# A sparse-attention and feed-forward kernel: a fifth room for raw w2, half of its low parts by GpSimd, and two pieces of w1 asked for later

## The chip, the cores and the metric

The kernel runs on one core of a Trainium2 chip. The metric is the device time of one execution in microseconds; three runs of the kernel before gave 777.71, 779.08 and 780.20 us, median 779.08 us.

## The reference

For 4 batches of 768 tokens and 8 heads of 64, block-sparse attention (blocks of 32 tokens; a query block sees its neighbours, the first and the last block and three sampled ones; the first and the last query block see all), then a feed-forward layer with a residual, all in float32:

```
x   = softmax(mask(q @ k.T / 8)) @ v                  # 3072 rows of 512
xn  = (x - mean) / sqrt(var + 1e-6) * g
out = x + relu(xn @ w1) @ w2                          # w1 512x2048, w2 2048x512
```

## The kernel before, in words

Weights reach the chip as float64 bit patterns. The kernel turns each piece into float32 with three integer passes on VectorE (lines 421, 423, 425), and then into a high and a low float16 part, since every feed-forward product is computed as three float16 matmuls (high by high, low by high, high by low). w1 has 8 pieces of 1 MB (`split_w1`), w2 has 16 of 0.5 MB (`split_w2`).

A piece of w1: VectorE makes the float32, ScalarE scales it in place (L433) and rounds it to the high part (L434), GpSimd subtracts for the low part (L435). A piece of w2: VectorE makes the float32, ScalarE scales and rounds in one step (L431), and VectorE makes the low part (L445, `low_w2`), one piece behind.

Raw pieces and float32 pieces lie in memory that has another use later (lines 405 to 410). Raw w1 has four rooms in the space of w2's parts; raw w2 has four: the second halves of `hh` and `hl` (called `late`) and the two `stg` tiles, which also hold float32 pieces of w1. The float32 pieces of w2 have two rooms, the output tiles `ot`. A load is issued from GpSimd's queue, right after the passes that free its room; the first four pieces of w1 are issued at the start (L508), the first four of w2 in step 2 (L521).

The attention is cut into 60 visits, 15 a batch. At first each pair of visits shares one job, the keys and values of four query blocks: visits 0 and 1 are job 0, 2 and 3 job 1, 4 and 5 job 2; visit 6 is a job of two blocks, and visits 7 to 10 are one job of the first and the last block. One job's transfers on SyncE's queue are, in this order: the band's keys (L144), the values (L180, L188), which must wait until the visits that used that buffer have read it, and twelve gathers of sampled key blocks (L153). The sampled values come by indirect transfers from GpSimd's queue (L192). There are two key and two value buffers.

All engines execute in the order in which the program is written. One pass of the main loop (line 553) is step s. It writes: scores of visit s on TensorE (L203), row maxima on VectorE (`biggest`, L239, L240), attention by values of visit s-1 on TensorE (L274) with its eviction on VectorE (L316 to L322), the exponentials of visit s on ScalarE (L252), and then a list of tasks: the next job's transfers (in even steps at first), the transposes of visit s (`turn`, L264), the weight pieces that `at(step, ...)` put there, and at the end the norm of a finished tile (`norm_a`: L336 to L343 and the subtraction for `xl` on GpSimd, L344). Between the tasks TensorE gets equal portions of the feed-forward work that is due (`run`). The feed-forward begins with step 4. Pieces 0 to 2 of w1 are split before step 0, 3 and 4 in step 0, 5 and 6 in step 1, 7 in step 2; w2 is split four pieces a step in steps 3 to 6.

Of the kernel before, what the change touches and what calls it, by code (L numbers as in the profile page):

```python
# [10 lines left out]
F16 = mybir.dt.float16  # L11
F32 = mybir.dt.float32
I32 = mybir.dt.int32
# [7 lines left out]
SW2 = 64.0  # L21
# [4 lines left out]
def sparse_attention_moe(  # L26
# [13 lines left out]
    nc = tc.nc  # L40
    P = 128
    B = qT.shape[0]
    NB, NR = 24, 3
# [4 lines left out]
    NX, LAG, FFN0 = 5, 1, 3  # L48

    const = ctx.enter_context(tc.tile_pool(name="const", bufs=1))  # L50
    sm = ctx.enter_context(tc.tile_pool(name="sm", bufs=4))
# [5 lines left out]
    def ring(name, n, shape, dtype):  # L57
        return [const.tile(shape, dtype, name=f"{name}{i}") for i in range(n)]
# [3 lines left out]
    w2h = const.tile([P, FT, DM], F16, name="w2h")  # L62
    w2l = const.tile([P, FT, DM], F16, name="w2l")
# [6 lines left out]
    x_s = ring("x", NX, [P, DM], F32)  # L70
# [6 lines left out]
    hl_s = const.tile([P, FT * 2 * P], F16, name="hl")  # L77
    ot_s = ring("ot", 2, [P, DM], F32)
    stg = ring("stg", 2, [P, 2048], F16)
    id_sb = const.tile([P, P], F32, name="id_sb")  # L80
    g_sb = const.tile([P, DM], F32, name="g_sb")
    eps = const.tile([P, 1], F32, name="eps")

    nc.scalar.add_instruction(
        mybir.InstLoadActFuncSet(
            name=nc.get_next_instruction_name(), act_func_set_id=ACT_SET, ins=[], outs=[]
        )
    )

    samp = const.tile([P, 2 * NB * NR], I32, name="samp")  # L90
    bid = const.tile([P, NB + 1], F32, name="bid")
    si = const.tile([P, NB, NR], I32, name="si")
    sf = const.tile([P, NB, NR], F32, name="sf")
    cf = const.tile([P, NB, NR], F32, name="cf")
    tf = const.tile([P, NB, NR], F32, name="tf")
    rf = const.tile([P, NB], F32, name="rf")
    rows = const.tile([P, NB], I32, name="rows")

# [201 lines left out]
    def evict(vi):  # L300
        n = 2 if vi.kind == "D" else 4
        u = vi.pv[:, 0 : n * 65].rearrange("p (h e) -> p h e", e=65)
        if vi.kind == "D":
            half = sm.tile([P, 2, 65], F32, tag="half", name=f"half{vi.i}")
            if not vi.r:
                nc.vector.tensor_copy(half, u)
                vi.half = half
                return
            wt = vi.st[:, 12:16].rearrange("p (r h) -> p r h", r=2).unsqueeze(3)
            nc.vector.tensor_mul(half, u, wt[:, 1].to_broadcast([P, 2, 65]))  # L310
            both = vi.mate.half
            nc.vector.tensor_mul(both, both, wt[:, 0].to_broadcast([P, 2, 65]))
            nc.vector.tensor_add(half, half, both)
            u = half
        rs = sm.tile([P, n, 1], F32, tag="rs", name=f"rs{vi.i}")
        nc.vector.tensor_scalar(out=rs, in0=u[:, :, D : D + 1], scalar1=1e-9, scalar2=None,  # L316
                                op0=ALU.add)
        nc.vector.reciprocal(rs, rs)
        x = vi.tile.x
        if vi.kind == "N":  # L320
            o = x[:, vi.hf * 256 : vi.hf * 256 + 256].rearrange("p (h d) -> p h d", d=D)
            nc.vector.tensor_mul(o, u[:, :, 0:D], rs.to_broadcast([P, 4, D]))  # L322
            return
        for rr in range(2):
            rows = slice(64 * rr, 64 * rr + 64)
            for pp in range(n // 2):
                h = 4 * (vi.hf if vi.kind == "D" else pp) + 2 * rr
                o = x[64:128, h * D : (h + 2) * D] if vi.kind == "D" else x[0:64, h * D : (h + 2) * D]
                nc.vector.tensor_mul(o.rearrange("p (j d) -> p j d", d=D),
                                     u[rows, 2 * pp : 2 * pp + 2, 0:D],  # L330
                                     rs[rows, 2 * pp : 2 * pp + 2, :].to_broadcast([64, 2, D]))
# [72 lines left out]
    split, s = {}, -1  # L404
    late = [x[:, FT * P :] for x in (hh_s, hl_s)]
    w2f, w2g = (x.rearrange("p f e -> p (f e)") for x in (w2h, w2l))
    raw1 = [w2f[:, 0:4096], w2f[:, 4096:8192], w2g[:, 0:4096], w2g[:, 4096:8192]]
    con1 = [stg[0], stg[1], late[0], late[1]]
    raw2 = [late[0], late[1], stg[0], stg[1]]
    con2 = [x.bitcast(F16) for x in ot_s]  # L410

    def load_w1(i, dma):
        dma.dma_start(raw1[i % 4].bitcast(I32), w1[i].bitcast(I32))

    def load_w2(i, dma):
        dma.dma_start(raw2[i % 4].bitcast(I32), w2[i].bitcast(I32))

    def split_w(raw, con, dh, dl, sw):
        raw = raw.bitcast(I32).rearrange("p (e t) -> p e t", t=2)
        wf = con.bitcast(I32)  # L420
        nc.vector.tensor_scalar(out=wf, in0=raw[:, :, 1], scalar1=3, scalar2=0x3FFFFFFF,  # L421
                                op0=ALU.logical_shift_left, op1=ALU.bitwise_and)
        nc.vector.scalar_tensor_tensor(out=wf, in0=raw[:, :, 1], scalar=-0x40000000, in1=wf,  # L423
                                       op0=ALU.bitwise_and, op1=ALU.bitwise_or)
        nc.vector.scalar_tensor_tensor(out=wf, in0=raw[:, :, 0], scalar=29, in1=wf,  # L425
                                       op0=ALU.logical_shift_right, op1=ALU.bitwise_or)
        wf = con.bitcast(F32)
        if len(dh.shape) == 3:
            wf = wf.rearrange("p (c f) -> p c f", c=CT)
        if sw == SW2:  # L430
            nc.scalar.activation(dh, wf, AF.Copy, scale=sw)  # L431
            return
        nc.scalar.activation(wf, wf, AF.Copy, scale=sw)  # L433
        nc.scalar.copy(dh, wf)  # L434
        nc.gpsimd.tensor_sub(dl, wf, dh)  # L435
# [6 lines left out]
            load_w1(i + 4, nc.gpsimd)  # L442

    def low_w2(i):
        nc.vector.scalar_tensor_tensor(out=w2l[:, i, :], in0=con2[i % 2].bitcast(F32), scalar=SW2,  # L445
                                       in1=w2h[:, i, :], op0=ALU.mult, op1=ALU.subtract)
        split[2, i] = s

    def split_w2(i):
        split_w(raw2[i % 4], con2[i % 2], w2h[:, i, :], w2l[:, i, :], SW2)  # L450
        for k in range(max(0, i - 1), i + i // 15):
            low_w2(k)
        if i + 4 < 16:
            load_w2(i + 4, nc.gpsimd)

    tiles, units, visits = [], [], []
    for b in range(B):
# [3 lines left out]
    n = 0  # L461
    while n < len(tiles):
        k = 1 if n == 0 or n == len(tiles) - 1 else 2
# [35 lines left out]
    def at(step, fn, *args):  # L499
        todo.setdefault(step, []).append((fn, args))  # L500
# [4 lines left out]
    nc.scalar.dma_start(bid, blocks)  # L505
    nc.scalar.dma_start(id_sb, eye)
    nc.scalar.dma_start(g_sb, g.to_broadcast([P, DM]))
    for i in range(4):  # L508
        load_w1(i, nc.gpsimd)
    nc.vector.memset(eps, 1e-6)  # L510
    nc.vector.memset(rf, 0.0)
# [2 lines left out]
        pass  # L514
    index_b()
    values(jobs[0])
    for i in range(3):
        split_w1(i)
    for i in range(3, 8):
        at((i - 3) // 2, split_w1, i)  # L520
    for i in range(4):  # L521
        at(2, load_w2, i, nc.gpsimd)
    for i in range(16):
        at(3 + i // 4, split_w2, i)
# [3 lines left out]
    queue, nextu, s = [], 0, 0  # L528
# [24 lines left out]
    while s < NV + LAG + 2 or queue or nextu < len(units):  # L553
        assert s < NV + 60
        vi = visits[s] if s < NV else None
# [27 lines left out]
        if vi:  # L583
# [7 lines left out]
            if queue:  # L591
                k = len(tasks) // 2
# [63 lines left out]
```

## Time and profile before

| what | value |
|---|---|
| median of three runs | 779.08 us |
| the profiled execution, device time | 781.21 us |
| its span, first to last instruction | 779.3 us |
| mean granted TensorE clock | 0.965 |
| busy share TensorE matmul, VectorE, ScalarE, GpSimd | 90%, 42%, 35%, 24% |

Times below are microseconds from the start of the span. PE is TensorE, PEld its weight load, DVE VectorE, ACT ScalarE, POOL GpSimd, SP SyncE, whose queue issues most transfers. L203 is line 203. "[8.25 <-PE ps L203]" behind an instruction says that its engine had been idle for 8.25 us and what ended that. A granted clock of 1.00 is 2.4 GHz, 0.50 is 1.2 GHz.

### The profile page before, as it was taken

Reading aid. Unit: us, or ns where it says so; the run is one execution under the profiler, and the core shown is the slowest. Engines: PE = TensorE matmul, PEld = TensorE weight load, DVE = VectorE, ACT = ScalarE, POOL = GpSimd, SP = SyncE. Lnnn points to the kernel's source line nnn. Section 1 sums busy time; section 2 is a strip of 40 time slices with the busy share of each in tenths; the row PEclk is TensorE's granted clock in tenths of the full one; section 3 lists DMA queues with packets and bytes.
Section 4 is the critical chain, followed back from the end, with each engine's and each line's share of the span. In section 5 each row is a group of like instructions: output and inputs, shape, how many; then the busy total and the mean of one; then the engine's idle time right before and its main releaser. Section 6 shows DMA issues by size and latency. Waiting matters only on the chain.

```text
span 779.3 us, 21817 instructions
## 1 busy us (share of the span) xinstructions
PE 702.4 (90%) x9344; PEld 475.1 (61%) x9344; DVE 326.2 (42%) x658; ACT 271.9 (35%) x561; POOL 188.1 (24%) x220
## 2 busy tenths in 40 slices
PE   0445767999999999999999999999999999999997
PEld 0122653775775775865875856765856857757764
DVE  7577887343351333443432323444332333432211
ACT  2355344343342331443341523343423423342200
POOL 5565211133322203113421103115221012210000
PEclk9967877999999999999999999999999999999999
DMA  8989872767947355569855437379864247431000
GB/s 330 341 251 282 285 247 84 219 184 209 246 131 188 94 167 150 155 165 238 231 153 137 126 129 218 111 194 252 214 167 132 64 147 223 147 87 29 14 29 14
DMA packets 109792, 132.16 MB, mean 170 GB/s; under 512 B 34560, under 2 KB 80896, under 8 KB 108672
## 3 DMA queue, kind: packets, MB, share of 16 engines
q1 hardware_dynamic: 96848, 83.92, 40.5%
q0 software_dynamic: 12416, 46.51, 17.9%
q8 instruction: 74, 1.21, 0.7%
q10 hardware_dynamic: 432, 0.34, 0.1%
q14 instruction: 22, 0.18, 0.1%
HBM read 118.15 MB, written 6.29 MB: 160 GB/s over the span
## 4 chain that ended last, share of the span: by engine, by line
PE 71%; issue 13%; DMA 8%; DVE 5%; POOL 1%; SPq 1%; ACT 1%; POOLq 0%; DVEq 0%
PE pu L367 27%; PE pd L392 25%; PE ps L203 7%; PE pv L274 7%; PE pt L264 6%; DMA ks<-kT 5%; DMA vs<-v 3%; DVE ot L423 1%; DVE w2l L445 1%; DVE ot L421 1%; DMA samp<-sampled 1%; POOL xl L344 0%; DVE st L239 0%; DVE ot L425 0%; SPq L149 0%
## 5 line engine op out<-in xcount | busy, mean ns | idle before, releaser
L367 PEld LDWEIGHTS <-w1h 128*128 128x128 f16 x1664 | 153.6, 99 | 18.1 <-issue 0.2
L252 ACT ACTIVATE p<-ps,st 128x256 f32<-128x256 f32 (+1 forms) x208 | 85.9, 491 | 222.8 <-DVE rs L316 116.4
L392 PE MATMUL pd<-w2h,hl 128*128 128x512 f16 x384 | 147.0, 383 | 0.0
L392 PE MATMUL pd<-w2l,hh 128*128 128x512 f16 x384 | 147.0, 383 | 0.0
L392 PE MATMUL pd<-w2h,hh 128*128 128x512 f16 x384 | 146.9, 383 | 0.0
L378 DVE SCALAR_TENSOR_TENSOR hl<-pu,hh 128x512 f16<-128x512 f32 x96 | 66.4, 692 | 171.2 <-ACT hh L377 170.7
L392 PEld LDWEIGHTS <-hh 128*128 128x128 f16 x768 | 75.2, 99 | 84.7 <-issue 3.0
L367 PE MATMUL pu<-xth,w1h 128*128 128x256 f16 (+1 forms) x832 | 120.9, 267 | 0.0
L367 PE MATMUL pu<-xth,w1l 128*128 128x256 f16 (+1 forms) x832 | 120.9, 267 | 0.0
L367 PE MATMUL pu<-xtl,w1h 128*128 128x256 f16 (+1 forms) x832 | 120.8, 267 | 0.0
L203 PE MATMUL ps<-ks,q 64*32 64x256 f32 (+1 forms) x1664 | 73.5, 418 | 40.3 <-DMA ks<-kT 37.6
L239 DVE TENSOR_REDUCE st<-ps 128x4 f32<-128x1024 f32 (+1 forms) x60 | 69.0, 1151 | 93.5 <-PE ps L203 93.4
L192 POOL DMA_INDIRECT vs<-v,rows x88 | 86.9, 987 | 88.0 <-PE pv L274 49.4
L377 ACT ACTIVATE hh<-pu 128x512 f16<-128x512 f32 x96 | 57.5, 599 | 108.9 <-PE pu L367 108.5
L264 PE MATMUL pt<-id_sb,p 128*128 128x128 f32 x448 | 66.3, 289 | 27.3 <-ACT p L252 23.3
L398 DVE SCALAR_TENSOR_TENSOR ot<-pd,x 128x512 f32<-128x512 f32 x24 | 16.6, 690 | 160.3 <-PE pd L392 160.3
L367 PEld LDWEIGHTS <-w1l 128*128 128x128 f16 x832 | 78.5, 99 | 8.2
L265 ACT COPY pt<-pt 128x512 f32<-128x512 f32 x120 | 61.9, 564 | 61.2 <-PE pt L264 50.7
L264 PEld LDWEIGHTS pt<-id_sb,p 128*128 128x128 f32 x448 | 53.6, 147 | 39.2 <-ACT p L252 28.0
L274 PEld LDWEIGHTS pv<-vs,pt 128*32 128x32 f32 x3584 | 55.6, 110 | 33.9 <-issue 28.4
L400 POOL DMA_DIRECT2D out<-ot x24 | 14.0, 583 | 255.9 <-DVE ot L398 255.9
L203 PEld LDWEIGHTS ps<-ks,q 64*32 64x32 f32 x1664 | 27.1, 109 | 72.0 <-issue 37.1
(83 smaller groups left out, 454.0 us busy)
## 6 DMA issues: line engine op xcount, KB each, us to landing
ks<-kT SPq DMA_DIRECT2D x28, 768.0 KB
ks<-kT SPq DMA_DIRECT2D x264, 64.0 KB
vs<-v SPq DMA_DIRECT2D x20, 780.0 KB
vs<-v SPq DMA_DIRECT2D x4, 1560.0 KB
q<-qT SPq DMA_DIRECT2D x24, 256.0 KB
out<-ot POOLq DMA_DIRECT2D x24, 256.0 KB
vs<-v SPq DMA_DIRECT2D x16, 260.0 KB
w2h<-w POOLq DMA_DIRECT2D x4, 1024.0 KB
```

What stands on the lines that cost most here:

```text
L192: nc.gpsimd.indirect_dma_start(out=vs[:, 2 * gg, :], out_offset=None, in_=src, in_offset=bass.IndirectOffsetOnAxis(ap=rows[:, i : i + 1], ...
L203: nc.tensor.matmul(ps[32 * part : 32 * part + 32, col : col + n], lhs[64 * row : 64 * row + 64], rhs[64 * row : 64 * row + 64], start=True ...
L239: nc.vector.tensor_reduce(out=st[:, 0:n], in_=seen(vi), axis=AX.X, op=ALU.max, negate=True)
L252: nc.scalar.activation(p_s[:, h * w : (h + 1) * w], seen(vi)[:, h, :], AF.Exp, bias=vi.st[:, 4 + h : 5 + h], scale=0.125)
L264: nc.tensor.transpose(pt[:, k - lo, :], p_s[:, k * P : (k + 1) * P], id_sb)
L265: nc.scalar.copy(dst[:, lo:hi, :], pt[:, 0 : hi - lo, :])
L274: nc.tensor.matmul(pv[32 * row : 32 * row + 32, 65 * col : 65 * col + 65], pt[:, ch, 32 * row : 32 * row + 32], vs[:, vv, 65 * e : 65 * e ...
L367: nc.tensor.matmul(ph[:, j * n : (j + 1) * n], w[:, ct, fs], x[:, ct, 0:n], start=m == 0, stop=m == 3 * CT - 1, skip_group_check=True)
L377: nc.scalar.activation(dh, ph, AF.Relu)
L378: nc.vector.scalar_tensor_tensor(out=dl, in0=ph, scalar=0.0, in1=dh, op0=ALU.max, op1=ALU.subtract)
L392: nc.tensor.matmul(po, x[:, f, ts], w[:, f, :], start=m == 0, stop=m == 3 * FT - 1)
L398: nc.vector.scalar_tensor_tensor(out=ot, in0=po, scalar=1.0 / (SW1 * SW2), in1=t.x, op0=ALU.mult, op1=ALU.add)
```

## The change

The index scratch moves into a new 4 KB tile `room`, which afterwards is the fifth room for raw w2. The float32 pieces of w2 get a third room, the last `x` tile. Odd pieces of w2 go the way of w1: ScalarE scales in place and rounds, GpSimd subtracts for the low part; even pieces go as before, with the low part of piece i-1 written by VectorE behind the passes of odd piece i. Two pieces of w1 instead of four are issued at the start, the next two behind the first job's values; two instead of three are split before step 0, then two a step in steps 0 to 2. The first piece of w2 is issued in step 1, the next four in step 2, each later one five pieces ahead. The half sums of the two long query blocks get two fixed tiles.

```diff
@@ -77,8 +77,10 @@
+    room = const.tile([P, 2048], F16, name="room")
+    half_s = ring("half", 2, [P, 2, 65], F32)
@@ -87,12 +89,13 @@
-    samp = const.tile([P, 2 * NB * NR], I32, name="samp")
+    part = room.bitcast(I32)
+    samp = part[:, 0 : 2 * NB * NR]
+    sf, cf, tf = (part[:, (2 + k) * NB * NR : (3 + k) * NB * NR].bitcast(F32)
+                  .rearrange("p (n r) -> p n r", r=NR) for k in range(3))
...
-            half = sm.tile([P, 2, 65], F32, tag="half", name=f"half{vi.i}")
+            half = half_s[vi.r % 2]
@@ -406,16 +409,16 @@
-    raw2 = [late[0], late[1], stg[0], stg[1]]
-    con2 = [x.bitcast(F16) for x in ot_s]
+    raw2 = [room, late[0], late[1], stg[0], stg[1]]
+    con2 = [x.bitcast(F16) for x in (ot_s[0], ot_s[1], x_s[NX - 1])]
...
-        dma.dma_start(raw2[i % 4].bitcast(I32), w2[i].bitcast(I32))
-    def split_w(raw, con, dh, dl, sw):
+        dma.dma_start(raw2[i % 5].bitcast(I32), w2[i].bitcast(I32))
+    def split_w(raw, con, dh, dl, sw, vector=False):
@@ -427,7 +430,7 @@
-        if sw == SW2:
+        if vector:
             nc.scalar.activation(dh, wf, AF.Copy, scale=sw)
             return
         nc.scalar.activation(wf, wf, AF.Copy, scale=sw)
         nc.scalar.copy(dh, wf)
         nc.gpsimd.tensor_sub(dl, wf, dh)
@@ -442,16 +445,19 @@
-        nc.vector.scalar_tensor_tensor(out=w2l[:, i, :], in0=con2[i % 2].bitcast(F32), scalar=SW2,
+        nc.vector.scalar_tensor_tensor(out=w2l[:, i, :], in0=con2[i % 3].bitcast(F32), scalar=SW2,
...
     def split_w2(i):
-        split_w(raw2[i % 4], con2[i % 2], w2h[:, i, :], w2l[:, i, :], SW2)
-        for k in range(max(0, i - 1), i + i // 15):
-            low_w2(k)
-        if i + 4 < 16:
-            load_w2(i + 4, nc.gpsimd)
+        split_w(raw2[i % 5], con2[i % 3], w2h[:, i, :], w2l[:, i, :], SW2,
+                vector=i % 2 == 0)
+        if i % 2:
+            low_w2(i - 1)
+            split[2, i] = s
+        if i + 5 < 16:
+            load_w2(i + 5, nc.gpsimd)
@@ -505,7 +511,7 @@
-    for i in range(4):
+    for i in range(2):
         load_w1(i, nc.gpsimd)
@@ -514,11 +520,14 @@
     index_b()
     values(jobs[0])
-    for i in range(3):
+    for i in range(2, 4):
+        load_w1(i, nc.gpsimd)
+    for i in range(2):
         split_w1(i)
-    for i in range(3, 8):
-        at((i - 3) // 2, split_w1, i)
-    for i in range(4):
+    for i in range(2, 8):
+        at((i - 2) // 2, split_w1, i)
+    at(1, load_w2, 0, nc.gpsimd)
+    for i in range(1, 5):
         at(2, load_w2, i, nc.gpsimd)
```

## Rows read from the trace of the kernel before

**Rows 1.** The page: busy tenths in 40 slices of 19.5 us, and GB/s.

```profile
PE   0445767999999999999999999999999999999997
...
DMA  8989872767947355569855437379864247431000
GB/s 330 341 251 282 285 247 84 219 184 209 246 131 188 94 167 150 155 165 238 231 153 137 126 129 218 111 194 252 214 167 132 64 147 223 147 87 29 14 29 14
```

**Rows 2.** Stretches: length, PE, PEld, DVE, ACT, POOL busy, PEclk, DMA share, GB/s.

```profile
120.00:140.00 20.00, 15.16 (x157) 6.85 (x159) 13.25 (x27) 6.17 (x12) 6.14 (x7) 0.81 0.25 74
140.00:160.00 20.00, 19.92 (x319) 16.43 (x308) 9.00 (x25) 7.78 (x17) 3.00 (x5) 1.00 0.64 181
```

**Rows 3.** Waits from 82 to 140 us: who waited for whom, total, times, longest.

```profile
PE pt L264 <- ACT p L252: 17.5, 3, 9.2
...
DVE hl L378 <- ACT hh L377: 5.7, 4, 3.0
```

**Rows 4.** Timeline of DVE: the row maxima of visits 4 and 7.

```profile
81.36 1.22 DVE L239 TENSOR_REDUCE st<-ps 128x4 f32<-128x1024 f32 x1
...
130.77 0.95 DVE L239 TENSOR_REDUCE st<-ps 128x2 f32<-128x768 f32 x1
```

**Rows 5.** Groups from 70 to 132 us, by form: busy, mean ns, idle before.

```profile
L445 DVE SCALAR_TENSOR_TENSOR w2l<-ot,w2h 128x512 f16<-128x512 f32 x16 | 11.0, 685 | 0.1
L431 ACT ACTIVATE w2h<-ot 128x512 f16<-128x512 f32 x16 | 10.1, 630 | 31.9 <-DVE ot L425 31.9
...
L423 DVE SCALAR_TENSOR_TENSOR ot<-stg,ot 128x512 int32<-128x512 int32 x8 | 5.5, 693 | 0.3
...
L421 DVE TENSOR_SCALAR ot<-stg 128x512 int32<-128x512 int32 x8 | 3.5, 433 | 0.3
```

**Rows 6.** Timeline: subtractions on POOL and the passes of DVE beside them.

```profile
14.10 0.69 DVE L421 TENSOR_SCALAR stg<-w2h 128x1024 int32<-128x1024 int32 x1
...
14.82 1.23 DVE L423 SCALAR_TENSOR_TENSOR stg<-w2h,stg 128x1024 int32<-128x1024 int32 x1
...
16.98 2.31 POOL L435 TENSOR_TENSOR w1l<-stg,w1h 128x1024 f16<-128x1024 f32 x1
17.22 2.62 DVE L421 TENSOR_SCALAR hh<-w2l 128x1024 int32<-128x1024 int32 x1
...
19.87 3.34 DVE L423 SCALAR_TENSOR_TENSOR hh<-w2l,hh 128x1024 int32<-128x1024 int32 x1
19.99 2.14 POOL L435 TENSOR_TENSOR w1l<-stg,w1h 128x1024 f16<-128x1024 f32 x1
...
100.73 1.16 POOL L344 TENSOR_TENSOR xl<-xn,xh 128x512 f16<-128x512 f32 x1 [3.01 <-ACT xh L343]
...
101.17 1.00 DVE L421 TENSOR_SCALAR ot<-hh 128x512 int32<-128x512 int32 x1
```

**Rows 7.** The chain that ended last: start, length, what, up to step 4.

```profile
52.41 4.01 PE ps L203 x32
...
77.70 1.92 PE ps L203 x20
```

**Rows 8.** Timeline of DVE and POOL in steps 0 to 3.

```profile
32.72 1.23 DVE L239 TENSOR_REDUCE st<-ps 128x4 f32<-128x1024 f32 x1 [8.25 <-PE ps L203]
...
56.45 1.22 DVE L239 TENSOR_REDUCE st<-ps 128x4 f32<-128x1024 f32 x1 [5.14 <-PE ps L203]
...
58.53 0.68 DVE L421 TENSOR_SCALAR hl<-w2l 128x1024 int32<-128x1024 int32 x1
...
64.74 1.54 DVE L240 TENSOR_SCALAR st<-st 128x4 f32<-128x4 f32 x1
...
66.19 0.59 POOL L416 DMA_DIRECT2D hh<-w  x1
...
68.39 1.19 POOL L344 TENSOR_TENSOR xl<-xn,xh 128x512 f16<-128x512 f32 x1
...
72.14 0.43 DVE L421 TENSOR_SCALAR ot<-hh 128x512 int32<-128x512 int32 x1 [5.13 <-DMA hh<-w]
```

More of the change, by code (lines that the diff above doesn't have):

```diff
@@ L88, in sparse_attention_moe @@
     )
-    samp = const.tile([P, 2 * NB * NR], I32, name="samp")
+    part = room.bitcast(I32)
+    samp = part[:, 0 : 2 * NB * NR]
+    sf, cf, tf = (part[:, (2 + k) * NB * NR : (3 + k) * NB * NR].bitcast(F32)
+                  .rearrange("p (n r) -> p n r", r=NR) for k in range(3))
     bid = const.tile([P, NB + 1], F32, name="bid")
     si = const.tile([P, NB, NR], I32, name="si")
-    sf = const.tile([P, NB, NR], F32, name="sf")
-    cf = const.tile([P, NB, NR], F32, name="cf")
-    tf = const.tile([P, NB, NR], F32, name="tf")
     rf = const.tile([P, NB], F32, name="rf")
```

## The prediction

> **What bounds the kernel now.** I read the page's slices first: TensorE is busy nine tenths or more from the eighth slice on, about 140 us, and before that at 0 to 7 tenths [rows 1]. The stretches sharpen it: 15.2 of 20 us busy before 140 us, 19.9 of 20 after [rows 2]. So the time is a start of some 140 us and a saturated rest. All feed-forward work in steps 4 to 6 is dealt out by a plan that counts tasks, and the change leaves the number of tasks in those steps alone. TensorE therefore does the same work in the same order, and whatever the start gains or loses moves the end by as much. Removing busy time from an engine after 140 us would be worth nothing.
>
> The start has two stretches. In steps 4 to 6 TensorE waits for the exponentials, 17.5 us in three waits up to 9.2 [rows 3]; those wait for row maxima, and these stand on VectorE behind the four pieces of w2 of the step before. From the maximum of visit 4 to that of visit 7 it is 130.77 - 81.36 = 49.4 us, which VectorE fills [rows 4]. Before that the chain of work runs over transfers: the scores of visit 2 begin at 52.41 and creep for 4.0 us as keys arrive, and the last scores of visit 4 start at 77.70 [rows 7]. The DMA engines are eight or nine tenths busy in the first three slices [rows 1].
>
> **The change, part by part.** Let T2 be the moment when VectorE takes up the maximum of visit 2, 56.45 us now, where it had been idle for 5.14 us waiting for scores [rows 8].
>
> First, the order of the first transfers. It brings the first keys earlier: two pieces fewer stand ahead, 2 MB, and at 341 GB/s [rows 1] that is 6.1 us off the 8.25 us that VectorE waits for the first scores [rows 8]. But T2 hangs on the second job's keys, and by then the same transfers must have landed, all of w1 and both jobs, over engines that are already eight or nine tenths busy. Delayed pieces of w1 come between later keys instead. Three small terms remain: the first piece of w2, now asked for in step 1, adds 0.5 MB, 1.5 us at that rate; while the deferred w1 waits behind the first indirect transfers the queues may run short, up to 2 us; and one piece of w1 may slip behind the keys, -3.1 us. I take T2 1.0 us later, bounds -2.6 and +3.5.
>
> Second, steps 2 and 3. Step 2 now holds two pieces of w1 behind T2 where it held one: three passes, from 14.10 to 17.22, are 3.1 us [rows 6]. They were free before T2, in the idle time; now they aren't. The subtractions of those pieces block VectorE too (next part): now 1.4 us of it lands on the tiny operation after visit 3's maximum (1.54 us) [rows 8]; with two I count 0.6 us more, as part hides behind the norm. So VectorE reaches w2's piece 0 3.7 us later than now. There it waits 5.13 us for the raw piece today, until 72.14 [rows 8]. With that piece loaded in step 1 the wait is gone, and it starts 5.1 - 3.7 = 1.4 us earlier than now. Two things take this back. The `xl` subtraction at 68.39 [rows 8] fell into the idle time, and will fall on passes: 1.1 us. And pieces 1 to 4 are issued behind both subtractions, about 3.8 us later than 66.19; a load took 72.14 - 66.19 = 5.95 us to use [rows 8], so piece 1 comes 66.19 + 3.8 + 5.95 = 75.9, while VectorE is through piece 0 at 70.7 + 1.8 + 1.1 = 73.6. That is a wait of 2.3; with less traffic beside it I take 1.6, bounds 0 and 3. Sum of the part: -1.4 + 1.1 + 1.6 = +1.3.
>
> Third, the low parts. Eight of sixteen leave VectorE: 8 x 0.685 [rows 5] = -5.5 us, all of it inside steps 3 to 6, where VectorE is the path. In their place come eight subtractions on GpSimd. The trace shows what such a one does: while GpSimd subtracts (16.98 and 19.99, 2.31 and 2.14 us) VectorE's first pass takes 2.62 instead of 0.69 and its second 3.34 instead of 1.23, so 1.93 and 2.11 us are lost, nearly the whole subtraction [rows 6]. At the width of w2 one takes 1.16 us, and the pass beside it took 1.00 instead of 0.43, the rest falling on an eviction that reads PSUM [rows 5, 6]. So each costs between 0.57 and 1.16. By place: pieces 1, 5, 9 and 13 have a pass of the next piece right behind, 1.05 each; pieces 3, 7, 11 and 15 end a step, where maxima, norms or a wait for TensorE [rows 3] hide part, 0.6, 0.8, 0.3 and 0.8. Sum 6.7 us, bounds 4.6 and 9.3. The part costs 6.7 - 5.5 = +1.2. If the cover at the ends of steps is gone, it is +3.8.
>
> The Trainium skill, in "SBUF — State Buffer", section "SBUF: two separate sides", says that VectorE and GpSimd share a port pair, held by one instruction for its whole length, while the other blocks fully; it names VectorE's two-port modes and, against a GpSimd operation that reads SBUF, operations with two SBUF inputs. This trace agrees with the block (the 2.62 and 3.34 above). By the full block of 1.16 each the part would be 9.3 - 5.5 = +3.8; by the rows I stay at +1.2.
>
> ScalarE gets one more operation per odd piece, about 0.63 us [rows 5]. I cost it at nothing: it stood idle 31.9 us before those sixteen operations [rows 5]; without that cover it would be 8 x 0.63 = 5.0 us. The third float32 room only spares GpSimd's reader a collision. The fifth raw room buys the early first piece; later pieces have not been late, as the first passes over `stg` were preceded by 0.3 us of idle time in all [rows 5]. The scratch in `room`, the `half` tiles and the even pieces' branch change no instruction's length: nothing. The two deferred loads of w1 now stand on GpSimd's queue ahead of its first subtraction (16.98 [rows 6]), 2 x 0.59 us [rows 8] later for it and for the loads behind it; VectorE's wait of 8.25 us for the first scores covers that, and without it the 1.2 us would fall on the later pieces of w1.
>
> Sum: 1.0 + 1.3 + 1.2 = +3.5 us. The profiled execution, 781.21 us with a span of 779.3, stood 2.1 us over the median; I carry the sum to the median: 779.1 + 3.5 = 782.6 us.
>
> **The rivals.** A measurement of this kernel can tell about 0.3% from no change, 2.3 us: 776.7 to 781.4 is the same.
>
> Slower is my forecast. Its mechanism decides where w2's conversion reaches visit 7's maximum: the loss is there when that row stands later than 130.77.
>
> The keys' lead lasts (faster). If the second job's keys keep the whole 6.1 us that the first gain, the sum is -6.1 + 1.3 + 1.2 = -3.6: 775.5 us. It decides from T2 at 53.95 on, where the 2.5 us of the other two parts are paid. For it speaks that keys and w1 share the engines and the keys are now ahead; against it the engines' shares [rows 1], and that w1's loads still come before T2.
>
> GpSimd works beside VectorE without loss (faster). Then the low parts give -5.5, `xl` costs nothing: 1.0 + 0.2 - 5.5 = -4.3, 774.8 us. Against it stand two rows of 2.62 and 3.34 us [rows 6]; for it, nothing but that those were longer subtractions.
>
> The change does not do what it says (same). The early piece spares 5.13 us and the shorter VectorE work 5.5; if locks hide at 4.6 and the load of piece 1 is in time, with T2 unmoved: 0 - 0.3 - 0.9 = -1.2, 777.9 us. The two moves cancel in a queue that is full anyway.
>
> **How the numbers follow.** Chance for my forecast 0.58, for the lasting lead 0.13, for work without loss 0.06, for cancelling moves 0.23. So faster 0.19, same 0.23, slower 0.58. The forecast's own range comes from its bounds, which will not all fall on one side: 781.4 to 788.5 (T2 at +3.5, the wait at 3, the locks at 9.3 give +3.5 + 2.7 + 3.8 = 10, less the part that can't coincide). With the cases on the other side the range is 775.5 to 788.5.
>
> **What the profile after will show.** Right, if visit 0's maximum comes some 6 us before 32.72 while visit 2's stays within a few us of 56.45; if VectorE passes over 1 us long stand beside subtractions of 1.16 on GpSimd in steps 3 to 6; if the idle time of 5.13 is gone and a shorter one stands before piece 1; and if visit 4's maximum is 2 to 4 us later than 81.36 with the 49.4 us after it about as long. Wrong, if visit 2's maximum comes before 54, if passes keep 0.43 and 0.69 beside GpSimd, or if TensorE's order of work in steps 4 to 6 differs, which would break the rule that the rest only shifts.

## The result, and the profile after

The changed kernel takes 786.35 us in the median (783.66 to 787.75), the kernel before 779.08 us: a ratio of 1.0083 [1.0066, 1.0100], so 5.1 to 7.8 us slower. The profiled execution took 786.49 us with a span of 784.7. The forecast's sign holds, and the time lies in its range of 775.5 to 788.5. Its size does not: +3.5 us was forecast, +6.5 came by the ratio.

The page's first row of slices, TensorE's busy tenths:

```profile
PE   1415557799999999999999999999999999999997
```

The seventh and eighth slices, 117 to 157 us, stand at 7, where the eighth stood at 9 [rows 1]. The two stretches of [rows 2] show the same:

```profile
120.00:140.00 20.00, 14.07 (x216) 7.80 (x205) 16.79 (x29) 9.59 (x19) 4.38 (x6) 1.00 0.46 173
140.00:160.00 20.00, 16.64 (x223) 11.85 (x224) 9.47 (x25) 7.41 (x16) 7.51 (x9) 0.91 0.72 205
```

TensorE is busy for 30.7 of these 40 us instead of 35.1: the saturated part begins later. From visit 8 on nothing more is lost, as the maxima below show, so the whole loss lies in the start.

VectorE's timeline after (start, length, engine, line, operation, out<-in; in brackets the idle time ahead and what ended it). All lines of the changed kernel are some three higher than before.

```profile
22.90 1.23 DVE L242 TENSOR_REDUCE st<-ps 128x4 f32<-128x1024 f32 x1 [5.16 <-PE ps L206]
...
61.01 1.23 DVE L242 TENSOR_REDUCE st<-ps 128x4 f32<-128x1024 f32 x1 [14.50 <-PE ps L206]
...
71.05 1.68 DVE L343 SCALAR_TENSOR_TENSOR xn<-x,ln,g_sb 128x512 f32<-128x512 f32 x1
72.64 1.21 DVE L242 TENSOR_REDUCE st<-ps 128x4 f32<-128x1024 f32 x1
...
75.38 0.42 DVE L424 TENSOR_SCALAR ot<-room 128x512 int32<-128x512 int32 x1
...
78.92 0.43 DVE L424 TENSOR_SCALAR ot<-hh 128x512 int32<-128x512 int32 x1 [0.21 <-DMA hh<-w]
...
82.69 1.52 DVE L428 SCALAR_TENSOR_TENSOR x<-hl,x 128x512 int32<-128x512 int32 x1
...
86.02 0.43 DVE L424 TENSOR_SCALAR ot<-stg 128x512 int32<-128x512 int32 x1 [1.80 <-DMA stg<-w]
...
88.41 1.22 DVE L242 TENSOR_REDUCE st<-ps 128x4 f32<-128x1024 f32 x1
...
97.28 0.69 DVE L381 SCALAR_TENSOR_TENSOR hl<-pu,hh 128x512 f16<-128x512 f32 x1 [6.09 <-ACT hh L380]
...
141.24 0.94 DVE L242 TENSOR_REDUCE st<-ps 128x2 f32<-128x768 f32 x1
```

Visit 0's maximum comes at 22.90 instead of 32.72 [rows 8], 9.8 us earlier. By visit 2 the lead is gone: 61.01 against 56.45, after 14.5 us of waiting for scores.

One trace is not enough to say by how much. The kernel before was profiled a second time (experiment e6 below), and its T2 fell at 59.87, 3.4 us later than in the first trace. The first trace also holds three stands of TensorE, 1.2 us each, between 180 and 560 us, which the second and the changed kernel's don't; so the spans of the two traces shown first differ by 5.4 us only, while visit 8's maximum differs by 8.9. Against the second trace the difference is 6.42 us at visit 8 and 6.21 at the last visit (701.65 and 707.86), so that trace is the one to subtract. By stretches, from the row maxima:

| stretch | before | before, second trace | after | after less second trace | forecast |
|---|---|---|---|---|---|
| start to T2 (visit 2) | 56.45 | 59.87 | 61.01 | +1.1 | +1.0 |
| visit 2 to 3 | 7.03 | 7.53 | 11.63 | +4.1 | +3.7 |
| visit 3 to 4 | 17.88 | 17.32 | 15.77 | -1.6 | -2.1 |
| visit 4 to 7 | 49.41 | 49.22 | 52.83 | +3.6 | +0.9 |
| visit 7 to 8 | 9.74 | 9.02 | 8.14 | -0.9 | 0 |
| sum | 140.51 | 142.96 | 149.38 | +6.4 | +3.5 |

The forecast's terms are laid out by the same stretches: 3.7 is the second piece and its lock; -2.1 is the wait gone, less `xl`, less the wait for piece 1, with two of the eight low parts; 0.9 is the other six. Against this one trace the first three rows come out within 0.6 us; the last is off by 0.9. For T2 that is partly luck. Two more traces share their program up to T2 with one of the kernels: e2 with the kernel before (T2 at 58.88), e5 with the changed one (61.04). The means of 56.45, 58.88 and 59.87 and of 61.01 and 61.04 put T2 some 2.6 us later, not 1.1. The row of visits 4 to 7 is off by 2.7, and the waits from 80 to 145 us say where to look (who waited for whom: total, times, longest):

```profile
PE pt L267 <- ACT p L255: 18.4, 3, 9.2
...
DVE hl L381 <- ACT hh L380: 10.0, 4, 6.1
...
PE pu L370 <- DMA xth<-xh: 5.4, 1, 5.4
...
PE pu L370 <- DMA xtl<-xl: 3.9, 1, 3.9
```

The long waits of TensorE for the exponentials are as before, 18.4 against 17.5 [rows 3]. New are the last two: the first tile's up-projection waits for its own transposed input. VectorE's wait for the result grew from 3.0 [rows 3] to 6.1, and that is 3.1 of the 3.6 us.

Two rows of the chain of work name the transfers, one ahead of T2 and one ahead of that up-projection (start, length, what):

```profile
19.40 34.89 DMA vs<-v
...
78.17 13.55 DMA xtl<-xl
```

In the chain of the kernel before, the first of them is

```profile
28.29 21.23 DMA vs<-v
```

These are values of the second job. They are asked for 8.9 us earlier than before and land at 54.29, 4.8 us later than in the first trace (49.52) and 1.4 us later than in the second (52.89). SyncE's issues of the second job's last keys follow that landing in the chain, and T2 stands 6.7 us behind it, as before (6.9).

### The profile page after: what moved, and what is told of

Same layout as the page of the kernel before. It is cut to its first block, busy times and chain, and to the rows that moved or that the text cites. A ratio compares the mean times of both kernels' runs of the same rounds, so it can differ in the third digit from the quotient of the medians.

```text
span 784.7 us, 21818 instructions
## 1 busy us (share of the span) xinstructions
PE 697.2 (89%) x9344; PEld 475.0 (61%) x9344; DVE 324.2 (41%) x650; ACT 277.4 (35%) x569; POOL 198.4 (25%) x228
## 4 chain that ended last, share of the span: by engine, by line
PE 70%; issue 13%; DMA 8%; DVE 5%; POOL 2%; ACT 1%; SPq 1%; POOLq 0%; ACTq 0%
PE pu L370 27%; PE pd L395 25%; PE pv L277 6%; PE ps L206 6%; PE pt L267 5%; DMA vs<-v 4%; DMA ks<-kT 2%; DMA xtl<-xl 2%; DVE ot L428 1%; DVE ot L426 1%; POOL xl L347 1%; SPq L156 0%; DVE xn L343 0%; DVE w2l L448 0%; DVE st L242 0%
## 5 line engine op out<-in xcount | busy, mean ns | idle before, releaser
L206 PE MATMUL ps<-ks,q 64*32 64x256 f32 (+1 forms) x1664 | 71.0, 418 | 34.6 <-DMA ks<-kT 34.6
L277 PE MATMUL pv<-vs,pt 128*32 128x65 f32 x3584 | 66.2, 226 | 4.5 <-DMA vs<-v 2.8
```

The lines of the kernel that those rows point to most:

```text
L206: nc.tensor.matmul(ps[32 * part : 32 * part + 32, col : col + n], lhs[64 * row : 64 * row + 64], rhs[64 * row : 64 * row + 64], start=True ...
L277: nc.tensor.matmul(pv[32 * row : 32 * row + 32, 65 * col : 65 * col + 65], pt[:, ch, 32 * row : 32 * row + 32], vs[:, vv, 65 * e : 65 * e ...
```

## The experiments

The theory was, at first, the prediction's own: small losses in three places. The largest question was which part of the change carries them. Times are medians against the kernel before, run beside them on the same chip.

**e1: the order of w1 alone.**

```diff
-    for i in range(4):
+    for i in range(2):
         load_w1(i, nc.gpsimd)
...
-    for i in range(3):
+    for i in range(2, 4):
+        load_w1(i, nc.gpsimd)
+    for i in range(2):
         split_w1(i)
-    for i in range(3, 8):
-        at((i - 3) // 2, split_w1, i)
+    for i in range(2, 8):
+        at((i - 2) // 2, split_w1, i)
```

> The kernel before with the w1 order alone changed: two pieces asked for at the start, the next two behind the first job's values, two split before step 0 and two in each of steps 0 to 2. Theory A (the deferred pieces of w1 land among the second job's keys and values): visit 2's maximum moves from 56.45 to 60 to 62 us, and the time is 4 to 8 us over the kernel before. Theory B (the subtractions on GpSimd block VectorE and are the loss): within 2 us of the kernel before, as these are not in it.

785.97 us, ratio 1.0077 [1.0057, 1.0098]: +6.0 us, nearly all of the loss, from the order alone. T2 is at 61.83, visit 3 at 73.46 (11.63 later, as in the changed kernel). Against the second trace of the kernel before, its stretches are +2.0, +4.1, -0.9, +1.0 and -0.7: the second piece behind T2 and the later T2 are the loss. GpSimd's timeline has the loads of the last two pieces of w1, and the chain the values:

```profile
34.56 0.58 POOL L413 DMA_DIRECT2D w2l<-w  x1
...
40.02 0.72 POOL L413 DMA_DIRECT2D w2l<-w  x1
```

```profile
19.84 35.47 DMA vs<-v
```

For e9 below, one more row of e1: its four loads of w2 go out at 75.46 to 77.66, `xtl` at 78.87, and TensorE has it by 86.54, after 7.7 us at most.

```profile
86.54 0.59 PE L367 MATMUL pu<-xtl,w1h 128*128 128x128 f16 x4 [1.99 <-DMA xtl<-xl]
```

**e2: the low parts alone** (odd pieces' low halves by GpSimd, three f32 rooms).

```diff
-    con2 = [x.bitcast(F16) for x in ot_s]
+    con2 = [x.bitcast(F16) for x in (ot_s[0], ot_s[1], x_s[NX - 1])]
...
-        split_w(raw2[i % 4], con2[i % 2], w2h[:, i, :], w2l[:, i, :], SW2)
-        for k in range(max(0, i - 1), i + i // 15):
-            low_w2(k)
+        split_w(raw2[i % 4], con2[i % 3], w2h[:, i, :], w2l[:, i, :], SW2,
+                vector=i % 2 == 0)
+        if i % 2:
+            low_w2(i - 1)
+            split[2, i] = s
```

> The kernel before with the low parts of odd w2 pieces on GpSimd and the third float32 room, nothing else. Theory A: within 2 us of the kernel before, as eight operations of 0.685 us leave VectorE (-5.5) and eight blocks of about 0.8 us each come (5.7 to 6.7). Theory B: 5 to 8 us slower.

778.95 us, ratio 1.0003 [0.9991, 1.0015]: no change, with +1.2 forecast at the upper end of the interval. The lock is there, a subtraction on GpSimd and VectorE's pass beside it:

```profile
80.14 1.28 POOL L435 TENSOR_TENSOR w2l<-ot,w2h 128x512 f16<-128x512 f32 x1 [2.34 <-ACT w2h L434]
```

```profile
80.43 1.53 DVE L425 SCALAR_TENSOR_TENSOR x<-stg,x 128x512 int32<-128x512 int32 x1
```

1.53 instead of 0.69, and 1.52 to 1.54 at pieces 5, 9 and 13. Beside pieces 7 and 15 it is the norm that takes 1.63 instead of 0.75, beside piece 3 the tiny operation after visit 4's maximum, 0.80 instead of 0.36; beside piece 11 nothing is longer. That adds up to 5.6 us. VectorE gives away 8 x 0.685 = 5.5 us [rows 5], and the time agrees.

**e3: the fifth room and the early load alone.**

```diff
-    raw2 = [late[0], late[1], stg[0], stg[1]]
+    raw2 = [room, late[0], late[1], stg[0], stg[1]]
...
-    for i in range(4):
+    at(1, load_w2, 0, nc.gpsimd)
+    for i in range(1, 5):
         at(2, load_w2, i, nc.gpsimd)
```

> The kernel before with the fifth room for raw w2 and its earlier load alone, low parts all on VectorE, the old w1 order. Theory A: the wait of 5.13 us before piece 0 goes, but visit 4's maximum can come no earlier than its scores, 79.6 instead of 81.36, so -2 to +1 us. If the early load instead delays the second job's keys, visit 2's maximum comes 1 to 2 us later and the time is 0 to 3 us longer.

780.47 us, ratio 1.0025 [1.0010, 1.0040], some 2 us slower. The wait of 5.13 [rows 8], 3.4 in the second trace, moves to piece 1 and shrinks to this:

```profile
75.24 0.43 DVE L423 TENSOR_SCALAR ot<-hh 128x512 int32<-128x512 int32 x1 [1.74 <-DMA hh<-w]
```

Yet visit 3 to 4 takes 16.9 us instead of 17.3 to 17.9, and visits 4 to 7 take 50.4 instead of 49.2 to 49.4. What the wait gave is gone before visit 7. T2 is at 59.03, within what the unchanged program shows (56.45 to 59.87), so nothing can be said of the early load's effect on it.

**e4: the changed kernel with the old order of w1** (the reverse of e1's diff, applied to the changed kernel).

> The changed kernel with the old w1 order. Theory A: visit 2's maximum is back within 1 us of 56.45, and the time within 2 us of the kernel before. Theory B: still 5 to 8 us slower than the kernel before.

780.79 us, ratio 1.0022 [1.0010, 1.0035]. The rest of the change costs 1.7 us by itself; with e1's 6.0 that is 7.7, against 6.5 for the whole, which the intervals allow. T2 is at 58.07, not within 1 us of 56.45, but within the spread that e6 shows. Visits 3 to 7 take 68.4 us, against 66.5 and 67.3 in the two traces of the kernel before and 68.6 in the changed kernel. Yet TensorE does not wait for `xth` or `xtl` here: it waits 3.8 us, in two waits, for the third job's keys ahead of visit 4's scores.

**e6: the kernel before once more**, with no edit, profiled a second time.

> The kernel before once more, for a second trace of it. If its start varies from run to run, visit 2's maximum stands somewhere between 56 and 59 us; if the three stands of TensorE of 1.2 us in the first trace (one per batch, in the attention by values of visits 13, 28 and 43) belong to the kernel, they are here again; if to that one execution, they are not.

780.28 us, span 778.5. VectorE's maxima of visits 2, 4 and 7, and the chain's row:

```profile
59.87 1.22 DVE L239 TENSOR_REDUCE st<-ps 128x4 f32<-128x1024 f32 x1 [9.08 <-PE ps L203]
...
84.72 1.22 DVE L239 TENSOR_REDUCE st<-ps 128x4 f32<-128x1024 f32 x1
...
133.94 0.95 DVE L239 TENSOR_REDUCE st<-ps 128x2 f32<-128x768 f32 x1
```

```profile
29.69 23.20 DMA vs<-v
```

The same program, and T2 moves by 3.4 us with the landing of the values (52.89 instead of 49.52). The expected 56 to 59 us was too narrow. That is the uncertainty of any statement on T2 from one trace; whether the execution or the chip makes it was not tried.

**e7 and e8: the two halves of the order.** e7 has the late loads with the old splits, e8 the new splits with the old loads. e7's edit is

```diff
-    for i in range(4):
+    for i in range(2):
         load_w1(i, nc.gpsimd)
...
+    for i in range(2, 4):
+        load_w1(i, nc.gpsimd)
     for i in range(3):
         split_w1(i)
```

> The kernel before with the w1 loads alone moved: two at the start, two behind the first job's values; three pieces are still split before step 0. Theory A (the loads' place is the loss: while only short packets are under way the DMA engines move 250 to 300 GB/s instead of 380 to 420 between 12 and 28 us, and some 1.8 MB less has landed): visit 2's maximum 60 to 63 us, 5 to 9 us slower than the kernel before. Theory C (the splits' place is the loss, a second piece behind visit 2): within 2 us.

And e8:

```diff
-    for i in range(3):
+    for i in range(2):
         split_w1(i)
-    for i in range(3, 8):
-        at((i - 3) // 2, split_w1, i)
+    for i in range(2, 8):
+        at((i - 2) // 2, split_w1, i)
```

> The kernel before with the w1 splits alone moved: four loads at the start as before, but two pieces split before step 0 and two in each of steps 0 to 2. Theory A: visit 2's maximum stays at 56 to 59 us; the second piece behind it costs 3.1 us, of which the wait of 5.1 us before w2's piece 0 hides most if the loads come in time: 0 to 4 us slower. Theory C: 5 to 8 us slower.

e7: 780.62 us, ratio 1.0019 [1.0002, 1.0036], T2 at 58.68, visit 3 at 66.66. e8: 781.12 us, ratio 1.0032 [1.0020, 1.0044], T2 at 56.38, visit 3 at 68.00. Neither half is the loss: e7's theory A and e8's theory C had 5 to 9 and 5 to 8 us. Together (e1) they cost +6.0, by themselves +1.5 and +2.5; the intervals leave room for a plain sum, the traces speak against it. T2 is at 58.68 and 56.38 with one half, at 61.01 and 61.83 with both. In all nine traces of kernels without both halves it lies between 56.38 and 59.87, in all five with both between 61.01 and 64.29. The loads of the last two pieces of w1 on GpSimd, and the values in the chain, stand beside that. In e7:

```profile
37.62 0.57 POOL L413 DMA_DIRECT2D w2l<-w  x1
48.46 0.58 POOL L413 DMA_DIRECT2D w2l<-w  x1
```

```profile
19.77 29.77 DMA vs<-v
```

In e8:

```profile
43.26 0.58 POOL L413 DMA_DIRECT2D w2l<-w  x1
...
45.92 0.76 POOL L413 DMA_DIRECT2D w2l<-w  x1
```

```profile
29.34 16.46 DMA vs<-v
```

With the old splits the last load goes out when the values are nearly in (48.46, landing at 49.54). With the old loads both go out late, at most 2.5 us ahead of the values' landing at 45.80. Only with both edits do two megabytes go out within six microseconds well before that landing, in e1 at 34.56 and 40.02 with the values in at 55.31. So I read that what the order costs at T2 it costs by what it puts side by side at 35 to 52 us, and not by its first 28 us, which e7 shares. That it is these two loads which slow the values is read from five traces (these, the changed kernel and e10) and not shown: a kernel with those two loads alone moved was not tried, and the unchanged program's landing moves by 3.4 us too.

e8 also shows the second piece behind T2 by itself: visit 3 follows T2 by 11.62 us instead of 7.03 and 7.53, 4.1 to 4.6 us.

```profile
56.38 1.22 DVE L239 TENSOR_REDUCE st<-ps 128x4 f32<-128x1024 f32 x1 [4.18 <-PE ps L203]
...
68.00 1.21 DVE L239 TENSOR_REDUCE st<-ps 128x4 f32<-128x1024 f32 x1
```

**e5: the changed kernel, the first tile's norm ahead of four loads of w2** in step 2.

```diff
+    at(2, lambda: norms())
     for i in range(1, 5):
         at(2, load_w2, i, nc.gpsimd)
```

> The changed kernel with the norm of the first tile (with its subtraction on GpSimd and its two transposing transfers) ahead of the four w2 loads of step 2 instead of behind them. Theory D (the transposes, which landed at 91 us, compete with those loads and cost the 3.0 us by which the wait for the first up-projection in step 4 grew, 6.09 against 3.05): 2 to 4 us faster than the changed kernel, 782 to 784 us. If the transposes are late for another reason, within 1 us of the changed kernel's 786.35.

786.45 us, ratio 1.0092 [1.0064, 1.0120]: no gain. `xl` is computed at 74.69 instead of 76.98, and the wait stays (6.58 us), because the transposing transfer is as slow as it was:

```profile
77.98 13.43 DMA xtl<-xl
```

The edit did not do what it was meant to. SyncE issues the transfer behind the third job's gathers and `xth`, at 77.98 instead of 78.17, so it went out no earlier, and the loads of w2, now issued at 75.79 to 77.95, still go beside it. So e5 does not decide on theory D.

The last four were run on another chip, where the kernel before took 782.97 us (779.42 to 785.29). Ratios are to that.

**e9: two loads of w2 beside the transposes instead of four.** The changed kernel with its rooms in another order, so that three pieces of w2 can be asked for in step 1.

```diff
-    raw2 = [room, late[0], late[1], stg[0], stg[1]]
+    raw2 = [room, stg[0], stg[1], late[0], late[1]]
...
-    at(1, load_w2, 0, nc.gpsimd)
-    for i in range(1, 5):
-        at(2, load_w2, i, nc.gpsimd)
+    for i in range(5):
+        at(1 + i // 3, load_w2, i, nc.gpsimd)
```

> The changed kernel with its five rooms in another order (the fifth room, the two stg rooms, the two late rooms), and pieces 0, 1 and 2 of w2 asked for in step 1, pieces 3 and 4 in step 2, so that two loads of w2 instead of four are asked for right ahead of the first tile's transposing DMAs. Theory 'collision' (the wait of 6.1 us for the first normed tile is the transposes' transfer beside the loads of w2): the transposes land about as early as the control's, 78.3 to 80.6 after a like start, the wait of the low normed part falls from 6.1 to about 3 us, and 782 to 784 us. Rival 'the order alone' (the transposes wait for their tile's attention, not for w2): the wait stays at 5 to 6 us, and 785 to 787 us.

VectorE's timeline:

```profile
62.91 1.22 DVE L242 TENSOR_REDUCE st<-ps 128x4 f32<-128x1024 f32 x1 [15.89 <-PE ps L206]
...
94.64 0.69 DVE L381 SCALAR_TENSOR_TENSOR hl<-pu,hh 128x512 f16<-128x512 f32 x1 [3.90 <-ACT hh L380]
```

TensorE's first matmul over `xtl` waited until 91.77 in the changed kernel. Here it has no wait ahead of it:

```profile
85.39 0.63 PE L370 MATMUL pu<-xtl,w1h 128*128 128x128 f16 x4
```

The transfer, issued at 78.90, took 6.5 us at most instead of 13.55. The wait falls from 6.09 to 3.90, visits 4 to 7 take 50.6 us instead of 52.8, and visit 3 to 4 takes 13.4 instead of 15.8. So fewer loads beside it go with a quicker transfer. The four loads alone do not make it slow, as e1 has them too, with 7.7 us; and e10 below has the same 3.90 with all four loads. The time is 789.04 us, ratio 1.0074 [1.0055, 1.0093], not told apart from the change's 1.0083. T2 is 1.9 us later than in the changed kernel's trace, with two more loads on the way by then. Visit 7 to 8 takes 9.8 instead of 8.1, as in all four traces on this chip (9.79 to 9.84), e9's edit or not. Whether the later T2 comes from those loads or from the chance that e6 shows was not tried.

**e10: the changed kernel with one piece less behind T2** (pieces 4, 5 and 6 of w1 in step 1).

```diff
-        at((i - 2) // 2, split_w1, i)
+        at((0, 0, 1, 1, 1, 2)[i - 2], split_w1, i)
```

> The changed kernel with piece 3 of step 0's two... that is, steps 0, 1 and 2 hold pieces 2 and 3, pieces 4, 5 and 6, and piece 7, instead of two pieces each: one piece less behind T2. Theory 'two places': T2 within 1 us of the changed kernel's 61.0, or later by up to 3 us where the idle time before it does not take piece 6; visit 3 earlier by 1 to 4 us, and 783 to 785 us. Rival 'the loss is made at the start' (the stretch of 12 to 28 us in which the queues move less, not made up): T2 later by the 4.1 us of the piece, visit 3 unchanged, 786 to 787 us.

790.09 us, ratio 1.0076 [1.0054, 1.0098]. Visit 3 follows T2 by 7.85 us instead of 11.63, but T2 itself is 3.3 us later, and again it is the values:

```profile
19.85 36.57 DMA vs<-v
```

```profile
64.29 1.23 DVE L242 TENSOR_REDUCE st<-ps 128x4 f32<-128x1024 f32 x1 [11.39 <-PE ps L206]
```

VectorE idles 11.4 us and T2 comes with a landing at 56.42. Visit 3 is at 72.14 instead of 72.64: the theory of two places, which had wanted 1 to 4 us, gets half a microsecond, and the rival's picture is the nearer one.

e10 bears on e9 too. It leaves the four loads of w2 where the changed kernel has them (74.72 to 77.0), ahead of `xtl` at 79.72. Visits 4 to 7 take 50.4 us all the same, and VectorE's wait is e9's:

```profile
95.34 0.69 DVE L381 SCALAR_TENSOR_TENSOR hl<-pu,hh 128x512 f16<-128x512 f32 x1 [3.90 <-ACT hh L380]
```

TensorE waits elsewhere, for the third job's keys ahead of visit 4's scores, and by 90.91, when it first needs `xtl`, that has landed:

```profile
86.91 1.92 PE L206 MATMUL ps<-ks,q 64*32 64x256 f32 x20 [5.46 <-DMA ks<-kT]
```

**b2: the kernel before with piece 2 in step 0 and three pieces in step 1.** If late loads of pieces 6 and 7 and a single piece behind T2 are all that matters, this should have beaten both kernels.

```diff
-    for i in range(3):
+    for i in range(2):
         split_w1(i)
-    for i in range(3, 8):
-        at((i - 3) // 2, split_w1, i)
+    for i in range(2, 8):
+        at((0, 0, 1, 1, 1, 2)[i - 2], split_w1, i)
```

> The kernel before, its four pieces of w1 still asked for up front; of the splits, the third piece (piece 2) moves from ahead of the steps into step 0, and steps 1 and 2 hold pieces 4, 5, 6 and piece 7 instead of pieces 5, 6 and 7. So one piece still stands behind T2 as before, and the loads of pieces 6 and 7 are asked for some 7 us later. Theory 'two places' (the loss of the order is 4.1 us of a second piece behind T2, and loads of w1 that land among the gathers of the second job): T2 about 56.4 to 57 us as in e8_splits_late, visit 3 about 64 to 65 instead of 68.00, and 776 to 778 us in all. Rival 'the whole second stage is full' (what visit 2 or 3 gains is waited for at the next transfers): visit 3 as early, but visit 5 and later within 1 us of the control's, and 779 us.

787.87 us, ratio 1.0062 [1.0046, 1.0078], so 3.6 to 6.1 us slower, and both theories are wrong. The traces of VectorE and of GpSimd say where it goes:

```profile
51.96 2.62 DVE L421 TENSOR_SCALAR hh<-w2l 128x1024 int32<-128x1024 int32 x1
54.61 3.03 DVE L423 SCALAR_TENSOR_TENSOR hh<-w2l,hh 128x1024 int32<-128x1024 int32 x1
...
61.61 3.04 DVE L423 SCALAR_TENSOR_TENSOR hl<-w2l,hl 128x1024 int32<-128x1024 int32 x1
...
77.81 0.43 DVE L421 TENSOR_SCALAR ot<-hh 128x512 int32<-128x512 int32 x1 [7.94 <-DMA hh<-w]
```

```profile
63.51 3.16 POOL L168 COPY ks<-kg 128x512 f32<-128x512 f32 x2
...
70.68 0.95 POOL L192 DMA_INDIRECT vs<-v,rows  x1 [0.30 <-issue]
71.65 2.14 POOL L435 TENSOR_TENSOR w1l<-hl,w1h 128x1024 f16<-128x1024 f32 x1
73.72 0.60 POOL L416 DMA_DIRECT2D hh<-w  x1
```

Piece 6 fills the idle time ahead of T2, but two subtractions on GpSimd stretch its passes by 3.7 us (2.62 and 3.03 instead of 0.69 and 1.23). The piece takes 3.1 + 3.7 = 6.8 us where 4.2 were idle in e8, and T2 is at 58.83 instead of e8's 56.38. Then piece 7's subtraction stands on GpSimd's queue behind the third job's copies and four value gathers, and the first load of w2 behind that subtraction: 73.72 instead of 70.01 in e8. VectorE, with one piece less to do, waits 7.94 us for it.

**b3: b2's splits with the fifth room**, in e9's order and with e9's early loads, the low parts on VectorE; an attempt at a kernel faster than both.

> The kernel before with the fifth room alone, its rooms in the order of e9_w2_ahead, four pieces of w1 asked for up front, the splits in the steps of b2_piece4_later, and w2 pieces 0, 1 and 2 asked for in step 1, pieces 3 and 4 in step 2. Theory: T2 about 57, no wait of 5.1 us before piece 0 of w2, the transposes not late, and 772 to 777 us, faster than both kernels. Rival 'full queues' (a load that is taken earlier delays the second job's gathers or the transposes by as much): T2 at 59 to 61, 778 to 781 us.

785.66 us, ratio 1.0026 [1.0013, 1.0039], some 2 us slower than the kernel before, as its rival had it, and 2.2 us faster than b2. The wait for w2 is gone, and visit 4 comes at 83.09 instead of 87.03. But `xl` is computed at 75.75, behind the same late subtraction, and its transfer stands in the chain:

```profile
77.00 8.44 DMA xtl<-xl
```

Visits 4 to 5 take 20.5 us instead of b2's 18.4. No run here was faster than the kernel before beyond its interval.

## Why the prediction was right, and where not

**That the start sets the end** holds: from visit 8 to the last visit the distance to the second trace stays the same to 0.2 us. But the row that was to decide, visit 7's maximum later than 130.77, could not: it is at 141.24 in the changed kernel, and at 133.94 in the second trace of the kernel before. Visit 4's maximum, forecast 2 to 4 us later, is 7.1 us later than in the first trace and 3.7 than in the second.

**T2, +1.0.** Measured +1.1 against the second trace; +4.6 against the first, which is over the upper bound of +3.5; +2.6 by the means of three traces and two. That it is met by one of these is luck. The reading was right: the first keys' lead, 9.3 to 9.8 us and so more than the 6.1 reckoned, does not last, because T2 hangs on the second job. But the reason that the step named does not fit the traces: queues that run short early are not it (e7 has the same poor stretch, 285 and 270 GB/s in 12 to 20 and 20 to 28 us, and loses little), nor is the sum of bytes, as by 56 us the two kernels had moved as much (309 and 306 GB/s from the start on). What fits, and is not shown by a run of its own, is where the last two pieces of w1 fall. The step says that delayed pieces "come between later keys" and prices them by their bytes; it follows pieces 2 and 3, whose loads the diff moves, and not pieces 6 and 7, whose loads are issued by the splits that it moves.

**The second piece behind T2, 3.1 us, with 0.6 of lock.** Right: 11.63 - 7.53 = 4.1, of which the norm's 1.68 instead of 0.75 is 0.9, the lock's larger share. e8 shows it alone, with the old loads.

**w2's first pieces, -5.1 with +1.1 and +1.6 taken back.** Right in sum (-1.6 for the stretch, -2.1 forecast with two low parts), wrong in place: piece 1 waits 0.21 us, and 1.80 us of waiting stands ahead of piece 3; the pass beside `xl` takes 2.15 us instead of 0.69, so 1.46 where 1.1 was taken. The gain is smaller than it looks, as the wait of 5.13 was 3.4 in the second trace.

**The low parts, +1.2.** e2 leaves -0.7 to +1.2 us, likeliest 0. The locks were put at 6.7 us and are 5.6 by e2's rows: 0.84 at pieces 1, 5, 9 and 13, where 1.05 had been taken, and 2.2 instead of 2.5 at the ends of steps. The Trainium skill's rule of a full block ("SBUF — State Buffer", section "SBUF: two separate sides") agrees with the single row to 0.15 us: a pass that begins 0.3 us into a subtraction of 1.28 loses 0.84, where 0.99 of the subtraction was left. The +3.8 us that eight whole blocks would make are ruled out by e2's interval: here a pass begins behind the start of the subtraction, and beside piece 11 nothing is lost.

**The term that was missed.** Visits 4 to 7 were to take "about as long" and take 52.8 us instead of 49.2 to 49.4. The prediction counted the later issue of w2's pieces 1 to 4 as a wait for VectorE, 1.6 us, and did not ask what else is on its way at 75 to 79 us: the third job's keys and the first tile's transposes. In the changed kernel it is the transposes that come last, 13.55 us for `xtl`, and that TensorE waits for them there, 5.4 and 3.9 us, is shown. That wait of VectorE is 3.97 in e1, 3.58 in e3 and 4.23 in e4, so neither half of the change makes it alone.

That the four loads of w2 make `xtl` slow is not shown. e9, which takes two of them away, has it quicker; e1 has all four and a transfer of 7.7 us at most; e10 has all four and no wait for `xtl`; e5 did not move the transfer. Nor are the transposes the whole of the loss, as visit 4's maximum is a poor border. From visit 3 to visit 7, one trace each, the kernel before takes 67.3 and 66.5 us, the changed kernel 68.6, e4 68.4 and e10 67.1, and in the last two TensorE waits for the third job's keys and not for the transposes. So something of the third job or of the first tile comes late beside w2's loads, and which one differs by kernel. By these borders the stretch cost +2.1 us against the second trace, where -1.2 was forecast (-2.1 + 0.9). That difference of 3.3 us makes up the gap between +3.5 and +6.4; the other rows add 0.5 and take back 0.9.

**The rivals.** A lead that lasts fell with T2. GpSimd beside VectorE without loss fell with the passes of 1.52 us. Moves that cancel describe e2, the low parts alone, and not the change.

**What stays open.** e9 takes 4.6 us out of visits 3 to 7 in its trace and 0.7 out of the time, by the ratios; its T2 came 1.9 us later, and the intervals of the two ratios leave between 1.3 us lost and 2.7 gained. What makes `xtl` take 13.4 to 13.6 us in the changed kernel and in e5, and at most 8.5 in e1, e3, e4, e9 and b3, is open. A kernel that also moves the last two loads of w1 behind the second job's values was not tried.

## What to carry to other kernels

A step that converts a piece also asks for the next one: when its place in the order changes, follow the transfer that it issues, to the stretch where that lands, and look at who else's transfers are on the way there. An in-order queue that holds arithmetic, gathers and weight loads at once, as GpSimd's here, can make all of them late when one is moved (in b2 a load of w2 went out 3.7 us later than in e8), so a piece that fills idle time on VectorE can cost more than the idle time (b2). And before reading a loss of some us out of one trace, take a second trace of the unchanged kernel: T2 moved by 3.4 us here with no edit at all.

## What the runs showed that was not expected

The DMA engines can be as busy and move much less. From 12 to 28 us (length, five engines' busy time, TensorE's clock, the DMA engines' share, GB/s), before and after:

```profile
12.00:28.00 16.00, 2.70 (x12) 0.64 (x12) 12.30 (x8) 6.30 (x6) 10.84 (x9) 1.00 1.04 393
```

```profile
12.00:28.00 16.00, 7.49 (x64) 3.36 (x72) 7.17 (x8) 6.95 (x10) 14.27 (x15) 1.00 1.03 280
```

The share is 1.04 and 1.03, the rate 393 and 280 GB/s. GpSimd's queue, with w1's long rows, moved 4.96 MB in 853 packets there before and 2.23 MB in 474 after; SyncE's, with the keys' and values' short ones, 1.33 MB in 2007 packets before and 2.25 MB in 2535 after. The forecast reckoned with one rate of 341 for all.

The three stands of TensorE, 1.2 us each, in the first trace of the kernel before, came back in every one of the last four traces, on the other chip, whatever the kernel; b2's waits from 180 to 560 us have them as

```profile
PE pv L274 <- issue: 2.8, 3, 0.9
```

and the second trace of the kernel before has no such row. There the kernel before took 782.97 us instead of 779.1, 3.9 more. From visit 8 to the end these four traces take 639.0 us and the second trace of the kernel before 635.5, so the stands are 3.5 of that. They come with the chip or the hour and not with the kernel; their cause stays open.
